# A scan and gated feed-forward kernel: w_down and one token slab loaded by GpSimd's queue instead of SyncE's

## The chip, the cores and the metric

The kernel runs on 1 core of one Trainium2 chip. A core has five engines with queues of their own: TensorE (PE, matmuls), VectorE (DVE), ScalarE (ACT), GpSimd (POOL) and SyncE (SP), and 16 DMA engines that move data between the chip's main memory and the on-chip buffer. The metric is the device time of one execution in microseconds (us). A profile shows one execution, with its times counted from the start of its span.

## The reference

For 2048 tokens x of 512 channels, in bf16:

```
xn = (x - mean) / sqrt(var + 1e-5)                       # over the 512 channels
h_t = Lam_bar * h_(t-1) + xn_t @ B_bar                   # complex, 512 states, t = 0..2047
s  = 2 * real(h @ C^T) + xn * Dskip
g  = silu((gelu(xn @ w_gate) * (xn @ w_up)) @ w_down)    # 512 -> 1376 -> 512
out = x + s * g
```

Lam_bar and B_bar come from Lambda, B and log_dt. The time loop is a recurrence over all tokens; the feed-forward part has no order among tokens.

## The kernel before, in words

The tokens are cut into 4 slabs (s = 0..3) of 512, each of 4 tiles (m = 0..3) of 128 tokens. For a slab:

- Tokens lie in x_tok. ScalarE normalizes them into xna (L749; for slab 0 VectorE does it at L356), with row scales rs made by GpSimd: L288 and L289 once for each tile of slab 0, L737 and L738 for slab 1, L761 for slabs 2 and 3. One DMA transpose (L360) turns xna into xnT.
- The scan half, `half(s, h)`: PE multiplies xnT by BT (L532, four matmuls for each of 8 groups), ScalarE copies each group out of its PSUM bank (L534, into U), VectorE rotates, scans (L563) and rotates back into hst. BT holds the transposed real and imaginary parts of B, loaded by two DMA transposes at L236. In the order of the program, slab 0's first three groups use the real part alone, and the fourth is the first to use the imaginary part.
- The feed-forward half: PE multiplies by w_up and w_gate (L402 and L383 in slab 0, L434 afterwards), ScalarE applies gelu, VectorE forms the product `at`, a DMA transpose (L450) puts it into atT, one for each tile, and PE multiplies atT by w_down, held in wd (L466, 11 matmuls a tile, `down_pair`). For slab 0 the tiles of atT are transposed, and used by PE, in the order 0, 2, 1, 3.
- `y_tile(s - 1, m)`: PE multiplies hst by the scaled C (L482); VectorE multiplies by g (L487), adds x (L493); SP stores the rows (L498).

PSUM has 6 ring banks shared by most products, and two banks for y_tile. A product waits until its bank's former contents were read.

Loads. All large DMAs go through SP's queue, in SP's order: first the tokens of slab 0 and the weights w_up and w_gate (L213 and L222), then the last rows of w_down (L669, 96 KB), slab 1's tokens (L217), Drow (L670), and the transposes of BT and of slab 0's xna. Behind slab 0's first atT come the other rows of w_down (L668, 1280 KB: 10 rows of 1 KB for each partition) and the tokens of slab 2 (L217, 512 KB), then the other transposes of atT. GpSimd issues no DMA; ScalarE issues three tiny ones at the start.

Order. Each operation is a step added by `pl.add`; `Plan.run` emits them in the order of the list `ORDER`, so that each engine's queue has its steps in that order. The arguments svc, dma, rank, lag and the costs are planning data and are not used when the kernel is built. An engine takes its own queue strictly in order, and a step that waits holds those behind it.

Of the kernel before, what the change touches and what calls it, by code (L numbers as in the profile page):

```python
# [17 lines left out]
PE, ACT, DVE, POOL, SP = "PE", "ACT", "DVE", "POOL", "SP"  # L18
# [2 lines left out]
ORDER = (  # L21
    20, 21, 22, 23, 24, 0, 26, 25, 19, 17, 18, 16, 1, 39, 14, 15, 12, 13, 2, 41, 3, 4, 5, 27, 28, 29, 30, 33, 60, 32, 46, 45, 40, 61, 34, 31, 63, 42,
    65, 62, 64, 69, 68, 66, 67, 70, 71, 72, 73, 35, 36, 37, 50, 51, 52, 54, 48, 53, 49, 57, 56, 58, 137, 38, 6, 43, 44, 147, 7, 79, 76, 82, 74, 80,
    77, 81, 78, 75, 8, 95, 91, 85, 97, 86, 93, 87, 88, 92, 55, 84, 47, 138, 94, 83, 96, 198, 149, 199, 151, 135, 59, 98, 136, 153, 9, 103, 107, 99,
    101, 109, 111, 104, 119, 100, 115, 102, 117, 108, 110, 125, 123, 133, 131, 216, 220, 139, 217, 140, 106, 120, 90, 112, 127, 214, 221, 105, 116,
    134, 154, 218, 150, 113, 126, 118, 124, 89, 215, 114, 128, 219, 122, 141, 148, 121, 143, 222, 223, 129, 130, 142, 152, 10, 155, 160, 164, 179,
    161, 165, 224, 229, 144, 11, 162, 166, 181, 183, 163, 185, 227, 167, 226, 225, 180, 168, 169, 170, 172, 171, 173, 174, 175, 176, 177, 178, 156,
    132, 233, 275, 283, 280, 279, 182, 358, 186, 184, 234, 187, 158, 237, 238, 276, 282, 157, 235, 228, 241, 243, 258, 244, 259, 236, 277, 278, 281,
    284, 285, 159, 239, 245, 296, 264, 247, 240, 246, 292, 260, 242, 200, 201, 202, 265, 302, 262, 297, 311, 293, 261, 298, 248, 303, 317, 307, 204,
    188, 203, 205, 263, 300, 294, 312, 308, 322, 299, 301, 315, 326, 313, 295, 309, 189, 191, 286, 190, 192, 230, 206, 207, 208, 318, 352, 316, 330,  # L30
    332, 232, 231, 305, 304, 327, 341, 209, 210, 211, 310, 324, 314, 328, 331, 323, 337, 290, 325, 339, 345, 287, 329, 288, 289, 333, 146, 320, 193,
# [5 lines left out]
    372, 486, 493, 501, 497, 474, 373, 484, 384, 385, 388, 386, 387, 467, 368, 434, 537, 477, 523, 494, 519, 478, 498, 487, 495, 524, 499, 525, 526,  # L37
    520, 507, 483, 389, 468, 390, 488, 374, 489, 504, 391, 505, 392, 401, 402, 403, 405, 406, 449, 551, 539, 521, 508, 552, 522, 513, 514, 535, 538,
    536, 515, 509, 404, 408, 407, 409, 527, 528, 531, 530, 518, 532, 469, 485, 464, 553, 490, 506, 557, 555, 541, 558, 569, 563, 556, 540, 559, 542,
    554, 565, 561, 567, 564, 578, 619, 562, 560, 574, 570, 624, 625, 576, 620, 584, 575, 568, 566, 580, 577, 591, 585, 599, 582, 589, 583, 597, 579,  # L40
    593, 581, 595, 572, 598, 600, 614, 510, 529, 516, 533, 571, 491, 587, 621, 629, 630, 612, 511, 622, 586, 626, 635, 615, 594, 596, 610, 608, 592,
    590, 604, 606, 636, 613, 607, 609, 605, 611, 534, 543, 544, 617, 601, 545, 573, 517, 627, 512, 602, 631, 470, 649, 616, 547, 548, 546, 549, 550,
    637, 623, 588, 643, 641, 644, 603, 645, 628, 638, 632, 618, 647, 650, 648, 655, 656, 642, 651, 661, 662, 646, 666, 667, 671, 672, 639, 640, 633,
    634, 652, 657, 658, 663, 664, 668, 669, 673, 674, 653, 654, 659, 660, 665, 670, 675,
)


# [33 lines left out]
def kernel(  # L81
# [17 lines left out]
    nc = tc.nc  # L99
# [9 lines left out]
    NS = S // TS  # L109
    M = TS // P  # L110
    NFT = (F + P - 1) // P
# [3 lines left out]
    HD = D // 2  # L115
# [12 lines left out]
    def sb(name, shape, dt=BF16):  # L128
        return consts.tile(shape, dt, name=name)

    x_tok = sb("x_tok", [P, NS * M, D])
# [3 lines left out]
    wd = sb("wd", [P, NFT, D])  # L135
# [43 lines left out]
    def dve(n, emit, reads=(), writes=(), rate=1.0, base=DV, **kw):  # L179
        return pl.add(DVE, base + n / 960.0 / rate, emit, reads, writes, lag=0.13, **kw)  # L180

    def acts(n, emit, reads=(), writes=(), ptr=0, **kw):
        return pl.add(ACT, AC + 0.12 * ptr + n / 1200.0, emit, reads, writes, lag=0.16, **kw)

    def pe(n, cols, emit, reads=(), writes=(), **kw):
        return pl.add(PE, n * (cols + 6) / 2400.0, emit, reads, writes, lag=0.22, **kw)
# [4 lines left out]
    def dma(eng, issue, land, emit, reads=(), writes=(), **kw):  # L191
        return pl.add(eng, issue, emit, reads, writes, lag=land, **kw)

    TURN, SLAB = (3, 2.28, 1.5), (2, 1.5, 1.0)
    x_r = A_x[0].rearrange("(m p) d -> p m d", p=P)
# [6 lines left out]
    sp_last, sp_at = [], [0.72]  # L202
# [11 lines left out]
               [(nm, k, c) for k in range(k0, k1) for c in range(3) if c0 <= CH[c][0] < c1])  # L214

    def load_slab(s, **kw):
        dma(SP, 0.8, 4.0, lambda: nc.sync.dma_start(out=x_tok[:, s * M : (s + 1) * M, :], in_=x_r[:, s * M : (s + 1) * M, :]),  # L217
            writes=[("x", s, m) for m in range(M)], svc=SLAB, **kw)


    def load_x(m, end, landed):
# [13 lines left out]
    for ri, src in enumerate((A_B_re, A_B_im)):  # L235
        dma(SP, 2.0, 3.0, lambda ri=ri, src=src: nc.sync.dma_start_transpose(out=BT[:, ri, :, :], in_=src), writes=[("BT", ri)],  # L236
            after=list(sp_last), svc=TURN)
# [16 lines left out]
    for i, (t, v) in enumerate(((pv0[0:4, :], A_log_dt), (pv1[0:4, :], A_Lambda_im), (pv1[4:8, :], A_Lambda_re))):  # L254
        first = [dma(ACT, 0.48, 1.7, lambda t=t, v=v: A.dma_start(out=t, in_=v.rearrange("(k p) -> k p", p=P)),
                     writes=[("pv", i)], rank=900.0, not_before=0.8, after=first)]
# [216 lines left out]
    def y_part(s, m, c0, c1, bank, key, seed, e):  # L473

        w = c1 - c0
        ps = bank[:, 0:w]
        if seed:
            acts(w, lambda: act(out=ps, in_=sk[s % 2][:, m, c0:c1], func=AF.Copy), [("sk", s % 2, m)], [key])  # L478

        def f():  # L480
            for j in range(2 * NPT):
                T.matmul(ps, lhsT=hst[s % 2][:, j // NPT, j % NPT, m * P : (m + 1) * P], rhs=C2[:, j // NPT, j % NPT, c0:c1],  # L482
                         start=(j == 0 and not seed), stop=(j == 2 * NPT - 1), skip_group_check=True)
        pe(2 * NPT, w, f, [("hst", s % 2, 0), ("hst", s % 2, 1)] + C2S + ([key] if seed else []), [key])
        gi, b = g2s[s, m]
        if seed:
            dve(w, lambda: V.tensor_tensor(out=yg[e][:, c0:c1], in0=ps, in1=g2[gi][:, b, c0:c1], op=ALU.mult), [key, ("g2", gi, b)], [("yg", e, c0)])  # L487
        else:
            ys = tF[:, 0, c0:c1]
            dve(w, lambda: V.tensor_tensor(out=ys, in0=ps, in1=sk[s % 2][:, m, c0:c1], op=ALU.add), [key, ("sk", s % 2, m)], [("tF",)])  # L490
            dve(w, lambda: V.tensor_tensor(out=yg[e][:, c0:c1], in0=ys, in1=g2[gi][:, b, c0:c1], op=ALU.mult), [("tF",), ("g2", gi, b)], [("yg", e, c0)])
        o = 2 + m % 2 if s == NS - 1 and m >= M - 2 else m % 2
        dve(w, lambda: V.tensor_tensor(out=ot[o][:, c0:c1], in0=yg[e][:, c0:c1], in1=x_tok[:, s * M + m, c0:c1], op=ALU.add),  # L493
            [("yg", e, c0), ("x", s, m)], [("ot", o, c0)], rate=2.0)
        mg = s * TS + m * P
        cuts = (0, HD) if (NS - 2, M - 2) <= (s, m) < (NS - 1, M - 2) else (c0,)
        for lo, hi in zip(cuts, (*cuts[1:], c1)):
            dma(SP, 0.35, 1.5, lambda lo=lo, hi=hi: nc.sync.dma_start(out=out_td[mg : mg + P, lo:hi], in_=ot[o][:, lo:hi]), [("ot", o, c0)], [("out", s, m, lo)], svc=(2, 0.4, 0.9))  # L498

    def y_tile(s, m):  # L500
        i = y_n[0] % 2
        seed = True
        y_n[0] += 1
        if (s, m) == (NS - 1, M - 1):
            for h in range(2):
                r, ps = bank()
                y_part(s, m, h * HD, (h + 1) * HD, ps, ("bank", r), True, m % 2)
        else:
            y_part(s, m, 0, D, ybank[i], ("y", i), seed, m % 2)
# [154 lines left out]
    for m in range(M):  # L664
        first_gates(m)
    load_slab(1, after=sp_last)
    wd_r = B_w_down[0 : (NFT - 1) * P, :].rearrange("(k p) d -> p k d", p=P)
    dma(SP, 0.6, 6.7, lambda: nc.sync.dma_start(out=wd[:, 0 : NFT - 1, :], in_=wd_r), writes=["wd0"], after=sp_last, svc=(2, 3.7, 1.0))  # L668
    dma(SP, 0.5, 4.0, lambda: nc.sync.dma_start(out=wd[:FL, NFT - 1, :], in_=B_w_down[(NFT - 1) * P : F, :]), writes=["wd"], after=sp_last, svc=(2, 0.3, 1.0))  # L669
    dma(SP, 0.7, 3.0, lambda: nc.sync.dma_start(out=Drow[:], in_=A_Dskip.partition_broadcast(P)), writes=["Drow"], after=sp_last, svc=(2, 0.5, 1.0))  # L670
    tables()
# [42 lines left out]
    for pt in range(NPT):  # L714
# [3 lines left out]
            out=C2[:, 0, pt, :], in0=CT[:, 0, pt, :], scalar=cre[:, pt : pt + 1], in1=tF[:, 1, :], op0=ALU.mult, op1=ALU.subtract),  # L718
            ["coef", ("CT", 0), ("tF",)], [("C2", 0, pt)], base=0.13)
        dve(512, lambda pt=pt: V.scalar_tensor_tensor(  # L720
            out=C2[:, 1, pt, :], in0=CT[:, 1, pt, :], scalar=ncre[:, pt : pt + 1], in1=tF[:, 0, :], op0=ALU.mult, op1=ALU.subtract),
# [104 lines left out]
```

## Time and profile before

| | us |
|---|---|
| median of 3 runs | 179.11 |
| lowest, highest | 178.77, 179.53 |
| the profiled execution, whole | 179.47 |
| its span | 177.7 |
| PE busy in the span | 172.0 |
| VectorE busy | 156.3 |
| ScalarE busy | 125.4 |
| GpSimd busy | 12.0 |

The profiled execution has 1.8 us outside its span. TensorE's granted clock was 1.00 all through. "Busy" of PE counts pipelined matmuls. In lines of the timeline the first column is the start, the second the duration of the group (for a DMA, of the issue on its queue, not of the transfer), then engine, line, operation, output and input; a bracket gives the idle time before the group and what ended it. "SPq" is SP's own instruction queue. A line of waits has the total, the number and the longest.

### The profile page before, as it was taken

How to read it: one execution, taken by the hardware profiler on the slowest of the kernel's cores; microseconds unless marked ns; L12 is line 12 of the kernel's file. 1: busy time of each engine (PE TensorE's matmuls, PEld its weight loads, DVE VectorE, ACT ScalarE, POOL GpSimd, SP SyncE). 2: the span in 40 equal slices, each digit the busy share in tenths (PEclk: the TensorE clock that was granted, in tenths of full speed). 3: DMA queues.
4: the chain of work that ended last, by engine and by line, in shares of the span. 5: the costliest groups of instructions: out<-in, count | busy, mean ns of one | idle time of the engine just before them, and what ended most of it. 6: DMA issues, size and time to landing. Idle time of an engine off the chain costs nothing.

```text
span 177.7 us, 2414 instructions
## 1 busy us (share of the span) xinstructions
PE 172.0 (97%) x834; PEld 82.4 (46%) x850; DVE 156.3 (88%) x252; ACT 125.4 (71%) x240; POOL 12.0 (7%) x25
## 2 busy tenths in 40 slices
PE   8999999899999999999999999999999999999992
PEld 2555544344455544444445454444444455444451
DVE  3729999999598994999979999899999999999754
ACT  6789999797998999899578855373148618572240
POOL 2471040000200000000040000000000000000000
PEclk9999999999999999999999999999999999999999
DMA  5999999999000709414000075094000006527022
GB/s 149 351 374 201 167 247 308 172 203 207 0 0 0 190 10 181 103 59 81 0 0 6 18 112 129 29 193 85 0 0 0 0 30 151 75 50 143 21 78 78
DMA packets 48083, 18.66 MB, mean 105 GB/s; under 512 B 40296, under 2 KB 47048, under 8 KB 48072
## 3 DMA queue, kind: packets, MB, share of 16 engines
q1 hardware_dynamic: 48048, 18.52, 49.0%
q8 instruction: 6, 0.10, 0.3%
q14 instruction: 5, 0.04, 0.1%
q10 hardware_dynamic: 24, 0.00, 0.0%
HBM read 6.46 MB, written 2.10 MB: 48 GB/s over the span
## 4 chain that ended last, share of the span: by engine, by line
PE 81%; DVE 8%; DMA 6%; ACT 2%; issue 1%; POOL 0%; DVEq 0%
PE ring L434 31%; PE ring L466 20%; PE ybank L482 14%; PE ring L532 12%; DMA atT<-at 5%; PE ring L383 3%; ACT at L392 2%; DVE st L279 1%; DVE Q L624 1%; DMA x_tok<-in_A_x_dram 1%; DVE at L416 1%; DVE yg L487 1%; DVE tab L624 1%; DVE junk L493 1%; DVE sk L365 1%
## 5 line engine op out<-in xcount | busy, mean ns | idle before, releaser
L434 PEld LDWEIGHTS <-xnT 128*128 128x128 bf16 x288 | 28.2, 98 | 28.4
L466 PE MATMUL ring<-wd,atT 128*128 128x512 bf16 (+1 forms) x170 | 39.0, 379 | 1.1 <-DMA atT<-at 0.7
L434 PE MATMUL ring<-wg,xnT 128*128 128x512 bf16 (+1 forms) x143 | 31.4, 357 | 0.1
L434 PE MATMUL ring<-wu,xnT 128*128 128x512 bf16 (+1 forms) x141 | 31.2, 356 | 0.2
L532 PE MATMUL ring<-xnT,BT 128*128 128x512 bf16 x128 | 30.1, 379 | 0.0
L563 DVE TENSOR_TENSOR_SCAN Fs<-rho,ini,W 128x512 bf16<-128x512 f32 x24 | 29.7, 1270 | 0.1
L437 ACT ACTIVATE ub<-ring 128x512 bf16<-128x512 f32 (+1 forms) x36 | 19.2, 555 | 14.1 <-PE ring L434 14.0
L482 PE MATMUL ybank<-C,hst 128*128 128x512 bf16 x116 | 27.3, 379 | 0.2
L466 PEld LDWEIGHTS <-atT 128*128 128x128 bf16 (+1 forms) x176 | 17.1, 98 | 22.0 <-DMA atT<-at 1.2
L534 ACT ACTIVATE U<-ring 128x512 bf16<-128x512 f32 x32 | 18.3, 601 | 8.1 <-PE ring L532 8.1
L437 ACT ACTIVATE gt<-ring 128x512 bf16<-128x512 f32 (+1 forms) x36 | 19.5, 556 | 3.7 <-PE ring L434 3.5
L482 PEld LDWEIGHTS <-hst 128*128 128x128 bf16 x136 | 13.3, 98 | 14.0
L532 PEld LDWEIGHTS <-BT 128*128 128x128 bf16 x128 | 12.5, 98 | 14.7
L544 DVE TENSOR_TENSOR Q<-U,tab 128x4096 bf16<-128x4096 bf16 x8 | 18.3, 2290 | 1.0 <-ACT tab L631 0.7
L469 ACT ACTIVATE g<-ring 128x512 f32<-128x512 f32 x16 | 9.3, 594 | 13.6 <-PE ring L466 13.5
L544 DVE TENSOR_TENSOR Q<-Fs,tab 128x4096 bf16<-128x4096 bf16 x8 | 18.3, 2287 | 0.1
L487 DVE TENSOR_TENSOR yg<-ybank,g 128x512 bf16<-128x512 f32 x15 | 10.2, 685 | 5.4 <-PE ybank L482 5.3
L744 ACT ACTIVATE junk<-x_tok 128x512 bf16<-128x512 bf16 x16 | 10.0, 635 | 1.1 <-DMA x_tok<-in_A_x_dram 1.1
L478 ACT ACTIVATE ybank<-sk 128x512 f32<-128x512 bf16 x15 | 9.0, 602 | 1.7 <-DVE yg L487 1.6
L749 ACT ACTIVATE xna<-x_tok,nb,rs 128x512 bf16<-128x512 bf16 x12 | 9.6, 817 | 0.0
L402 PE MATMUL ring<-wg,W 128*128 128x512 bf16 (+1 forms) x47 | 9.4, 356 | 0.1
L563 DVE TENSOR_TENSOR_SCAN Fs<-rho,W 128x512 bf16<-128x512 f32 x8 | 9.3, 1210 | 0.1
(127 smaller groups left out, 170.5 us busy)
## 6 DMA issues: line engine op xcount, KB each, us to landing
x_tok<-in_A_x_dram SPq DMA_DIRECT2D x3, 512.0 KB, 9.0
wg<-in_B_w_gate_dram SPq DMA_DIRECT2D x1, 1376.0 KB, 8.5
wd<-in_B_w_down_dram SPq DMA_DIRECT2D x1, 1280.0 KB, 8.2
out_dram<-ot SPq DMA_DIRECT2D x10, 128.0 KB, 1.7
wu<-in_B_w_up_dram SPq DMA_DIRECT2D x4, 256.0 KB, 4.0
x_tok<-in_A_x_dram SPq DMA_DIRECT2D x4, 128.0 KB, 2.3
out_dram<-ot SPq DMA_DIRECT2D x8, 64.0 KB, 1.6
wu<-in_B_w_up_dram SPq DMA_DIRECT2D x1, 352.0 KB
```

What stands on the lines that cost most here:

```text
L402: T.matmul(ps[:, 0 : b - a], lhsT=xcT[:, k, m * P : (m + 1) * P], rhs=wt[:, k, a:b], start=(k == 0), stop=(k == KT - 1))
L434: T.matmul(ps[:, 0 : b - a], lhsT=xnT[:, s % 2, m, k, :], rhs=wt[:, k, a:b], start=(k == 0), stop=(k == KT - 1))
L437: acts(b - a, lambda: act(out=dst[:, a:b], in_=ps[:, 0 : b - a], func=AF.Copy if up else AF.Gelu_apprx_tanh), [("bank", r)], [key], table= ...
L466: T.matmul(ps[:], lhsT=atT[:fs, k, m * P : (m + 1) * P], rhs=wd[:fs, k, :], start=(k == 0), stop=(k == NFT - 1))
L482: T.matmul(ps, lhsT=hst[s % 2][:, j // NPT, j % NPT, m * P : (m + 1) * P], rhs=C2[:, j // NPT, j % NPT, c0:c1], start=(j == 0 and not seed ...
L487: dve(w, lambda: V.tensor_tensor(out=yg[e][:, c0:c1], in0=ps, in1=g2[gi][:, b, c0:c1], op=ALU.mult), [key, ("g2", gi, b)], [("yg", e, c0)])
L532: T.matmul(ps[:], lhsT=BT[:, ri, k, pt * P : (pt + 1) * P], rhs=xnT[:, s % 2, :, k, :], start=(k == 0), stop=(k == KT - 1))
L534: acts(512, lambda q=q, ri=ri, ps=ps: act(out=U[ui][:, ri, q, :], in_=ps[:], func=AF.Copy), [("bank", r)], [("U", ui, q, ri)])
L544: dve(4096, lambda: V.tensor_tensor(out=Qf, in0=src.unsqueeze(1).to_broadcast(WQ), in1=table, op=ALU.mult), reads, ["Q"], rate=2.0)
L563: pl.add(DVE, 1.12 if s == 0 else 1.185, lambda ri=ri, q=q, pt=pt, first=first: V.tensor_tensor_scan(out=Fs[:, ri, q, :], data0=rho[:, pt ...
L744: acts(512, lambda i=i, fn=fn, sc=sc, m=m: act(out=junk()[:], in_=x_tok[:, s * M + m, :], func=fn, scale=sc, accum_out=sx[:, s, i, m : m + ...
L749: acts(512, lambda m=m: act(out=xn[m], in_=x_tok[:, s * M + m, :], func=AF.Identity, scale=rs[:, s, m : m + 1], bias=nb[:, s, m : m + 1]), ...
```

## The change

- The load of w_down's first 1280 rows (`wd`, before at L668) and the load of slab 2's tokens are issued by GpSimd instead of SP. In `ORDER` their steps (132 and 275) stand directly behind step 153, slab 0's last row scale, and so in GpSimd's queue between the L289 of tile 3 and the L737 and L738 of slab 1. In SP's queue they are gone from between the first and the second atT of slab 0.
- The stores of tiles 0 and 1 of slab 2 are issued in two halves of 256 columns each, as those of the four tiles after them already were. SP's queue has two stores more for it.
- No other instruction changes its place on its engine, nor do the waits other than by the new number of the semaphores. One added line shifts the line numbers by one. Slabs 1 and 3 stay on SP.

```diff
 ORDER = (
...
-  ... 59, 98, 136, 153, 9, 103, 107, ...
+  ... 59, 98, 136, 153, 132, 275, 9, 103, 107, ...
...
     def load_slab(s, **kw):
-        dma(SP, 0.8, 4.0, lambda: nc.sync.dma_start(out=x_tok[:, s * M : (s + 1) * M, :], in_=x_r[:, s * M : (s + 1) * M, :]),
-            writes=[("x", s, m) for m in range(M)], svc=SLAB, **kw)
+        eng, nq = (POOL, nc.gpsimd) if s == 2 else (SP, nc.sync)
+        dma(eng, 0.8, 4.0, lambda: nq.dma_start(out=x_tok[:, s * M : (s + 1) * M, :], in_=x_r[:, s * M : (s + 1) * M, :]),
+            writes=[("x", s, m) for m in range(M)], dma=(2, 0.8, 1.5), **kw)
...
-        cuts = (0, HD) if (NS - 2, M - 2) <= (s, m) < (NS - 1, M - 2) else (c0,)
+        cuts = (0, HD) if NS * M - 8 <= s * M + m < NS * M - 2 else (c0,)
...
-    dma(SP, 0.6, 6.7, lambda: nc.sync.dma_start(out=wd[:, 0 : NFT - 1, :], in_=wd_r), writes=["wd0"], after=sp_last, svc=(2, 3.7, 1.0))
+    dma(POOL, 0.6, 6.7, lambda: nc.gpsimd.dma_start(out=wd[:, 0 : NFT - 1, :], in_=wd_r), writes=["wd0"], after=sp_last, dma=(2, 0.8, 3.7))
```

## The prediction

> **What bounds the kernel now.** I read the page first: busy time by engine, and the DMA line of the 40 slices.
>
> ```profile
> PE 172.0 (97%) x834; PEld 82.4 (46%) x850; DVE 156.3 (88%) x252; ACT 125.4 (71%) x240; POOL 12.0 (7%) x25
> ...
> DMA  5999999999000709414000075094000006527022
> ```
>
> TensorE (PE) is busy in 172.0 of 177.7 us, and the DMA engines are full from 4.4 to 44 us (nine slices of 4.44 us), which is where the change works. Next I asked who waited on PE; the whole answer is two lines.
>
> ```profile
> PE ybank L296 <- PEq L810: 0.8, 1, 0.8
> PE ring L466 <- DMA atT<-at: 0.7, 1, 0.7
> ```
>
> The first is the start. The second is the only stall after it. PE's timeline from 17 us shows where:
>
> ```profile
> 24.11 7.07 PE L532 MATMUL ring<-xnT,BT 128*128 128x512 bf16 x32
> 31.22 2.54 PE L466 MATMUL ring<-wd,atT 128*128 128x512 bf16 x10
> 34.46 4.93 PE L466 MATMUL ring<-wd,atT 128*128 128x512 bf16 x22 [0.71 <-DMA atT<-at]
> ```
>
> From 34.46 PE runs without a gap to 172.7 us; the last stores end the span at 177.7. So a stall put in before 34 us is paid in full at the end, and the most that loads can give back is 0.71 us. What feeds this stretch is SP's queue and, in the changed kernel, POOL's. SP's timeline (start, duration of the issue):
>
> ```profile
> 15.61 3.08 SPq L360 DMA_TRANSPOSE xnT<-xna  x1
> 18.74 2.20 SPq L236 DMA_TRANSPOSE BT<-in_A_B_im_dram  x1
> 21.04 1.92 SPq L450 DMA_TRANSPOSE atT<-at  x1
> 23.01 0.58 SPq L668 DMA_DIRECT2D wd<-in_B_w_down_dram  x1
> 23.63 0.70 SPq L217 DMA_DIRECT2D x_tok<-in_A_x_dram  x1
> 25.21 8.34 SPq L450 DMA_TRANSPOSE atT<-at  x2
> 33.65 2.17 SPq L360 DMA_TRANSPOSE xnT<-xna  x1
> ```
>
> POOL's, around the new place of the two loads, which is behind the L289 of 14.64:
>
> ```profile
> 14.64 0.55 POOL L289 TENSOR_TENSOR rs<-ve,mhalf 128x1 f32<-128x1 f32 x1
> 22.98 0.24 POOL L737 TENSOR_SCALAR mq<-mv 128x4 f32<-128x4 f32 x1 [7.78 <-DVE mv L280]
> 23.30 1.84 POOL L738 TENSOR_TENSOR rs<-mq,mhalf 128x4 f32<-128x4 f32 x1
> ```
>
> And the windows of one us (last columns: DMA share, GB/s):
>
> ```profile
> 18.00:19.00 1.00, 1.00 (x6) 1.00 0.15 24
> 19.00:20.00 1.00, 1.00 (x9) 1.00 1.27 290
> 20.00:21.00 1.00, 1.00 (x7) 1.00 1.10 202
> ...
> 24.00:25.00 1.00, 1.00 (x7) 1.00 0.64 130
> ...
> 27.00:28.00 1.00, 1.00 (x7) 1.00 0.99 338
> ```
>
> Transposes move 240 GB/s (mean of the five windows from 19 to 24), plain loads 334 (mean of 26 to 30), and the engines are nearly empty from 18 to 19. From the issues and their times to landing: xnT of slab 0 lands at 15.61 + 6.1 = 21.7, BT's second half (BT_im) at 18.74 + 4.9 = 23.6, wd at 23.01 + 8.2 = 31.2, atT of token tile 2 at 25.21 + 9.2 = 34.4, slab 2 at about 32.5 (ScalarE's L744 waits 1.14 us and starts at 32.58).
>
> **Part 1: the stall that goes.** atT of tile 2 was queued at 25.21 behind wd and slab 2, 1.8 MB. Its issue stays at 25.21: SP waited there for VectorE's product, which ends at 25.19, so the 0.58 and 0.70 us of SP time saved bring nothing. Without that queue it lands in 3.5 to 4.1 us (the other atT rows), at about 29.3, before PE asks at 33.75. Gain: 0.71 us. Next late would be tile 1's atT, due at 33.76 + 2.54 = 36.3; it was in time even behind the queue. ScalarE's 1.14 us wait for slab 2 goes too, worth 0, since PE never waits for ScalarE in this trace. wd itself was due at 31.22 and landed at 31.2; moved up it has room.
>
> **Part 2: the stall that may come.** POOL reaches the loads at 15.19 (end of L289; neither waits for anything). Their bytes flow from about 16.2 (estimate: half of the 2.13 us from the first load's issue at 0.72 to its landing at 2.85). From then on they share the 16 DMA engines with the rest of BT_re, with xnT and with BT_im, which before had them alone. Who waits: the first matmul of L532 needs xnT at 24.11, slack 24.11 - 21.7 = 2.4. In program order three groups of four L532 matmuls use only BT_re, the fourth is the first with BT_im: at 24.11 + 3 x 0.864 = 26.70, slack 3.1.
>
> The work: BT_re has about 0.28 MB left at 16.2 (the 229 and 100 GB/s windows of 16 to 18), 1.2 us at 240 GB/s. xnT and BT_im are 0.524 MB each, 2.2 us each. Check on before: xnT's issue ends at 18.69; 18.69 + 2.2 + 2.2 + 0.55 to land = 23.64, as seen. The plain 1.83 MB need 5.5 us at 334 GB/s. No row of before has two queues with heavy traffic, so I bound it by how the engines might be shared:
> - No slowing, transposes leave gaps enough: stall 0.
> - Equal bytes: each side gets 1/(1/240 + 1/334) = 140 GB/s, a transpose takes 3.75 us. From 18.69, xnT lands at 23.0 (in time), BT_im at 18.69 + 7.5 + 0.55 = 26.75: stall 0.05.
> - Equal time: a transpose takes 4.4 us. xnT lands at 23.65 (in time), BT_im at 28.0: stall 1.3.
> - Plain loads first: 16.2 + 5.5 + 1.2 + 2.2 + 0.55 = 25.65 for xnT: stall 1.5; BT_im at 27.85 is then in time (due 28.24).
> - Plain first at the price they had in SP's queue, 7.3 us (atT of tile 0 landed about 25.2, slab 2 at 32.5): xnT at 27.45, stall 3.3.
>
> I take 1.0, between equal bytes and equal time but nearer the latter: the one issue made under plain traffic, the first of the two atT at 25.21, took 2.62 us where the same issue alone takes 1.40, so slowing by about two is what a row shows. Range of this term 0 to 3.3.
>
> The Trainium skill, "DMA: Bandwidth & Descriptors", section "Issuing engines are not separate DMA queues", says that transfers started by different engines run on the same 16 DMA engines and interleave, and that a second issuing engine saves only issue time. By that rule the no-slowing end falls away and the sum lies at the equal-bytes row or above.
>
> **Part 3: POOL's time.** Issuing on POOL is not in the trace. Low bound: SP's own issues of these two, 0.58 + 0.70 = 1.28 us; high bound: the longest issue in the trace twice, BT_re's 7.54 us, 15.1. Behind the loads on POOL stand L737 and L738, slab 1's row scales; ScalarE's L749 waits for those, and behind it in ScalarE's order the L534 copies that free PE's banks. Cover: POOL sat idle 7.8 us from 15.19 to 22.98. Then the third L534 ends at 28.37, and PE wants its bank for the eighth L532 group at 24.11 + 7 x 0.864 = 30.16: another 1.8. Up to 9.6 us for both issues cost nothing; I take the low end (same loads, nearest row), so 0.
>
> **Part 4: stores in halves.** Tiles 8 and 9 (slab 2) get one more SP issue each, 0.33 to 0.78 us (store rows after 140 us), ahead of slab 3's atT of tiles 1 and 3. The later of these is issued at 160.37 and lands 3.5 us on, at 163.9; PE wants it as its fourth down tile at 158.0 + 3 x 2.38 = 165.1. Slack 1.2 against at most 0.78: cost 0. Without that cover it would cost up to 0.78.
>
> **Sum.** The profiled execution took 179.47 us, 177.7 of span and 1.8 around it; that is 0.36 above the median of 179.11, so I apply differences to the median. -0.71 + 1.0 + 0 + 0 = +0.3: 179.4 us, a span near 178.0.
>
> **The rivals.**
> A, the loads slip in unseen. For it: the empty windows at 18 and 24. Against: everything else from 15 to 25 shows a DMA share at or above 1. Stall 0 to 0.4, time 178.4 to 178.8. More than 0.71 it cannot give, as PE has no other gap.
> B, transposes suffer more than by two. For it: BT_re's issue took 7.54 us while wg, slab 1 and others drained ahead of it; that queueing could return across queues. Against: its own queue was the full one there. Stall 1.6 to 3.3: 180.0 to 181.7.
> C, slower by POOL: writing requests for 1280 + 512 rows holds POOL past 24.8 us. It decides from 9.6 us for both issues. At 15.1, POOL gets to L737 at 30.3, the scales are ready at 32.5, L749 and the third L534 end at 34.2: PE's eighth group waits 4.0 and the second down tile 0.3 more for the fifth L534. -0.71 + 4.3 = +3.6: 182.7. Against it: SP's issue of these very loads took 1.28.
> D, VectorE keeps POOL from writing the requests while it works. VectorE runs from 15.23 to 30.2 almost without a gap; loads that start at 30.2 put wd at 30.2 + 8.2 = 38.4 where PE wants it at 31.22: +7.2 - 0.71, or 185.6. Against it: L738 ran wholly beside VectorE's work and was stretched to 1.84 us, from the 1.01 that L761's same operation took; it was not held to the end of that work. The Trainium skill warns of such a hold in "SBUF — State Buffer", section "SBUF: two separate sides": a 2-port VectorE operation locks GpSimd out while it writes descriptors. [...]
>
> **How the numbers follow.** A measurement of this kernel can tell about 0.5%, 0.9 us: 178.2 to 180.0 is no change. Forecast, stall 0.4 to 1.6, 178.8 to 180.0: 0.37, all within. A 0.25, of which 0.06 is measured more than 0.9 faster (the three runs of before scatter by 0.76) and 0.19 within. B 0.21, C 0.13 and D 0.04, all slower. Faster 0.06, same 0.56, slower 0.38. The range goes from A's end less scatter, 178.3, to B's end, 181.8; outside lie the low part of A, most of C and D, together under 0.2.
>
> **What would show it.** Right: wd and slab 2 land before 29 us; no PE wait at L466; one PE wait of about 1 us at L532, for xnT or BT_im; L737 still near 23.0. No wait at L532 is A; one above 1.6 is B; a late L737 with ScalarE waiting at L749 is C; wd landing after 31 is D. Wrong altogether: a new gap on PE after 40 us, or a tail that moves by more than 0.3 us.

## The result, and the profile after

| | before | after |
|---|---|---|
| median, us | 179.0 (6 runs, 178.77 to 179.53) | 185.37 (6 runs, 183.7 to 187.94) |
| profiled execution, us | 179.47 | 185.53 |
| its span, us | 177.7 | 183.7 |

The ratio is 1.031, with a 95% interval of 1.026 to 1.036: slower by 5.5 us, where the prediction said 179.4 and at most 181.8. Ratios leave out executions more than 1.5% above the fastest of their kernel (here 187.22 and 187.94), medians do not: by the medians it is 6.4 us.

The page of the changed kernel: the engines (busy, share, instructions), TensorE's granted clock in 40 slices of 4.59 us, the two DMA queues (packets, MB, share of 16 engines), and the two moved loads with the time from issue to landing.

```profile
PE 175.1 (95%) x850; PEld 83.3 (45%) x850; DVE 156.3 (85%) x252; ACT 125.3 (68%) x240; POOL 13.9 (8%) x27
...
PEclk9999997899999999999999999999999999999999
...
q1 hardware_dynamic: 46512, 16.68, 43.6%
q0 software_dynamic: 480, 1.84, 3.6%
...
wd<-in_B_w_down_dram POOLq DMA_DIRECT2D x1, 1280.0 KB, 11.1
...
x_tok<-in_A_x_dram POOLq DMA_DIRECT2D x1, 512.0 KB, 11.5
```

PE is busy for longer, 175.1 instead of 172.0 us. A part of this is the clock, which is low in the seventh and eighth slices, 27.6 to 36.7 us; another part may be missing records, since the profile before has 834 of the 850 matmuls. GpSimd's queue is a queue of its own, q0, and the profile calls it a software queue; SP's transposes and stores are q1.

PE's waits after (total, number, longest; the line numbers are higher by one than before):

```profile
PE ring L533 <- DMA xnT<-xna: 4.6, 1, 4.6
PE ybank L297 <- PEq L811: 0.8, 1, 0.8
```

The stall at w_down (0.7 us before) is gone; in its place stands one for xnT of slab 0, of 4.6 us. PE's timeline after:

```profile
29.49 8.75 PE L533 MATMUL ring<-xnT,BT 128*128 128x512 bf16 x32 [4.58 <-DMA xnT<-xna]
38.08 7.30 PE L467 MATMUL ring<-wd,atT 128*128 128x512 bf16 x33
45.22 2.75 PE L533 MATMUL ring<-xnT,BT 128*128 128x512 bf16 x12
```

Two things to see: the 32 matmuls begin at 29.49 instead of 24.11, and they take 8.75 us instead of 7.07. From 38 us PE runs without a gap. SP's queue and GpSimd's after (start, duration of the issue):

```profile
16.24 6.31 SPq L361 DMA_TRANSPOSE xnT<-xna  x1
22.60 6.36 SPq L237 DMA_TRANSPOSE BT<-in_A_B_im_dram  x1
29.06 4.93 SPq L451 DMA_TRANSPOSE atT<-at  x3
```
```profile
15.78 1.18 POOL L669 DMA_DIRECT2D wd<-in_B_w_down_dram  x1
16.96 0.78 POOL L218 DMA_DIRECT2D x_tok<-in_A_x_dram  x1
23.61 0.24 POOL L738 TENSOR_SCALAR mq<-mv 128x4 f32<-128x4 f32 x1 [5.88 <-DVE mv L281]
```

xnT's issue takes 6.31 us (3.08 before) and xnT lands 13.1 us after its start, at 29.4 (6.1 and 21.7 before). wd lands at 15.78 + 11.1 = 26.9, slab 2 at 16.96 + 11.5 = 28.5. The windows of one us of the changed kernel (length, PE busy and its matmuls, granted clock, DMA share, GB/s):

```profile
17.00:18.00 1.00, 1.00 (x7) 1.00 0.36 63
18.00:19.00 1.00, 1.00 (x6) 1.00 1.74 115
19.00:20.00 1.00, 1.00 (x8) 1.00 0.90 121
20.00:21.00 1.00, 1.00 (x8) 1.00 0.59 196
21.00:22.00 1.00, 1.00 (x7) 1.00 1.00 337
...
26.00:27.00 1.00, 0.00 (x0) 1.00 1.47 111
27.00:28.00 1.00, 0.00 (x0) 1.00 1.26 44
...
31.00:32.00 1.00, 1.00 (x4) 0.50 1.10 200
32.00:33.00 1.00, 1.00 (x4) 0.50 1.06 205
33.00:34.00 1.00, 1.00 (x6) 0.85 1.16 207
```

PE is idle from 26 to 28 (0.00, no matmul). The DMA engines move little at both ends of the loads, 63 to 196 GB/s from 17 to 21 us and 111 and 44 from 26 to 28, and PE's clock is at half from 30 to 33.

**Where the 6.0 us of span went.** 0.64 is in the head: the same L384 group starts at 6.37 instead of 5.73, before any changed instruction has run, so it is scatter. The first scan matmul comes at 29.49, 4.74 later than 24.11 + 0.64. From it to the next slab's first L533 (45.22) it is 15.73 us, 15.12 before: 0.61 more. The scan group takes 1.48 more to the first L467 (8.59 for 7.11), the slow clock; from there on it is 0.87 less, the 0.71 stall and some small gaps. The sum is 5.99; PE's last group starts at 178.53 instead of 172.54, which is 5.99 too.

### The profile page after: what moved, and what is told of

The parts are those of the page before. It is cut to its first block, busy times and chain, and to the rows that moved or that the text cites. A ratio compares the mean times of both kernels' runs of the same rounds, so it can differ in the third digit from the quotient of the medians.

```text
span 183.7 us, 2435 instructions
## 1 busy us (share of the span) xinstructions
PE 175.1 (95%) x850; PEld 83.3 (45%) x850; DVE 156.3 (85%) x252; ACT 125.3 (68%) x240; POOL 13.9 (8%) x27
## 3 DMA queue, kind: packets, MB, share of 16 engines
q0 software_dynamic: 480, 1.84, 3.6%
## 4 chain that ended last, share of the span: by engine, by line
PE 87%; DMA 7%; ACT 2%; DVE 2%; POOL 0%; issue 0%; DVEq 0%
PE ring L435 30%; PE ring L467 21%; PE ring L533 16%; PE ybank L483 14%; DMA xnT<-xna 7%; PE ring L384 3%; ACT at L393 2%; PE ring L297 1%; DVE yg L488 1%; PE ybank L297 1%; DVE junk L494 1%; ACT junk L353 0%; PE ybank L329 0%; PE ring L314 0%; POOL rs L290 0%
## 5 line engine op out<-in xcount | busy, mean ns | idle before, releaser
L467 PE MATMUL ring<-wd,atT 128*128 128x512 bf16 (+1 forms) x176 | 39.3, 379 | 0.0
L533 PE MATMUL ring<-xnT,BT 128*128 128x512 bf16 x128 | 31.8, 395 | 4.6 <-DMA xnT<-xna 4.6
L564 DVE TENSOR_TENSOR_SCAN Fs<-rho,ini,W 128x512 bf16<-128x512 f32 x24 | 29.7, 1270 | 0.1
L438 ACT ACTIVATE ub<-ring 128x512 bf16<-128x512 f32 (+1 forms) x36 | 19.2, 555 | 14.1 <-PE ring L435 14.0
L467 PEld LDWEIGHTS <-atT 128*128 128x128 bf16 (+1 forms) x176 | 17.2, 98 | 20.8
L533 PEld LDWEIGHTS <-BT 128*128 128x128 bf16 x128 | 12.9, 101 | 20.8 <-issue 7.3
L366 DVE TENSOR_TENSOR sk<-xna,Drow 128x512 bf16<-128x512 bf16 x16 | 6.5, 412 | 4.7 <-ACT xna L750 4.7
## 6 DMA issues: line engine op xcount, KB each, us to landing
wd<-in_B_w_down_dram POOLq DMA_DIRECT2D x1, 1280.0 KB, 11.1
x_tok<-in_A_x_dram POOLq DMA_DIRECT2D x1, 512.0 KB, 11.5
```

Of the source, the lines that this page charges most:

```text
L438: acts(b - a, lambda: act(out=dst[:, a:b], in_=ps[:, 0 : b - a], func=AF.Copy if up else AF.Gelu_apprx_tanh), [("bank", r)], [key], table= ...
L467: T.matmul(ps[:], lhsT=atT[:fs, k, m * P : (m + 1) * P], rhs=wd[:fs, k, :], start=(k == 0), stop=(k == NFT - 1))
L533: T.matmul(ps[:], lhsT=BT[:, ri, k, pt * P : (pt + 1) * P], rhs=xnT[:, s % 2, :, k, :], start=(k == 0), stop=(k == KT - 1))
L564: pl.add(DVE, 1.12 if s == 0 else 1.185, lambda ri=ri, q=q, pt=pt, first=first: V.tensor_tensor_scan(out=Fs[:, ri, q, :], data0=rho[:, pt ...
```

## Experiments

The first theory was the prediction's own, that transposes and loads share the 16 engines; its rivals were the stores in halves, GpSimd's issue time, the kind of queue, and the clock. Times are medians, ratios are to the kernel before on the same chip with their 95% intervals. An edit is shown against the kernel before, but that of `e4_act_queue`, `e6_pool_late`, `e7_after_fill`, `e9_slab3_pool` and `e13_after_fill26` against the changed kernel, that of `e8_act_big` against `e4_act_queue`, and that of `e11_wd_first` against `e10_slab_behind`. The change's stores in halves are in `e1_halves`, `e7_after_fill`, `e12_after_again` and `e13_after_fill26` alone.

### The parts by themselves

**Stores in halves alone** (`e1_halves`): the changed kernel with both loads back in their places on SP. Against the kernel before:

```diff
-        cuts = (0, HD) if (NS - 2, M - 2) <= (s, m) < (NS - 1, M - 2) else (c0,)
+        cuts = (0, HD) if NS * M - 8 <= s * M + m < NS * M - 2 else (c0,)
```

> Kernel before with the two more stores in halves only; both loads stay on SP. Theory 1 (the loads on GpSimd's queue get ahead of xnT's transpose on the shared DMA engines; the stores do nothing): 179.0 us within 0.5, PE's waits as before (0.7 at L466). Theory 2 (GpSimd's software queue itself, whatever its load, is what costs): the same, 179.0. A part of the 5 us from the stores would show here as a new wait or a longer tail after 140 us.

Measured: 179.25 us, ratio 1.0017 [0.9997, 1.0037]. The stores cost nothing that can be told.

**wd alone on GpSimd's queue** (`e2_wd_pool`): step 132 behind 153, slab 2 stays on SP.

```diff
-    dma(SP, ... nc.sync.dma_start(out=wd[:, 0 : NFT - 1, :], ...
+    dma(POOL, ... nc.gpsimd.dma_start(out=wd[:, 0 : NFT - 1, :], ...
```

> Kernel before with only wd's load (1.31 of the 1.83 MB) moved to GpSimd behind slab 0's row scales. Theory 1: xnT's landing moves by the bytes ahead of it, 7.0 x 1.31/1.83 = 5.0 us against 2.4 us of slack: PE waits about 2.6 us at L532, total 181 to 182 us. Theory 2: a cost that belongs to the queue and not to the bytes, so the same 4.6 us wait and 184 us as with both loads.

Measured: 183.55 us, ratio 1.0226 [1.0162, 1.029]. PE's waits in its profile (of an execution of 184.88 us, longer than the median):

```profile
PE ring L532 <- DMA xnT<-xna: 4.0, 1, 4.0
```

wd by itself makes most of the wait, in this execution more than the 2.6 us that its share of the bytes would give.

**Slab 2 alone on GpSimd's queue** (`e3_slab_pool`): step 275 behind 153, wd stays on SP.

```diff
-        dma(SP, ... nc.sync.dma_start(out=x_tok[...
+        eng, nq = (POOL, nc.gpsimd) if s == 2 else (SP, nc.sync)
+        dma(eng, ... nq.dma_start(out=x_tok[...
```

> Kernel before with only slab 2's load (0.52 of the 1.83 MB) moved to GpSimd. Theory 1: xnT moves by 7.0 x 0.52/1.83 = 2.0 us, inside its 2.4 us of slack: no wait at L532, and the 0.7 us wait at L466 shrinks, since tile 2's atT stands behind wd alone: 178.2 to 179.0 us. Theory 2: the same wait at L532 as with both loads, above 182 us.

Measured: 180.36 us, ratio 1.0075 [1.0046, 1.0103]. PE's waits, and the packets by queue between 20 and 22 us:

```profile
PE ring L467 <- DMA wd<-in_B_w_down_dram: 2.3, 1, 2.3
```
```profile
q1 hardware_dynamic: 48, 0.01, 47.4%
q0 software_dynamic: 9, 0.03, 6.0%
```

xnT is in time (15.98 + 8.4 = 24.4), but its issue still holds SP for 6.23 us. So SP issues wd at 26.09 instead of 23.01, it lands at 33.9, and PE waits for that. For two us in which xnT is under way only 48 of its packets end, while nine stragglers of the software queue finish.

### The same bytes in other queues

**Both loads on ScalarE's queue**, issued at 15.7 and 16.1 us (`e4_act_queue`):

```diff
-        eng, nq = (POOL, nc.gpsimd) if s == 2 else (SP, nc.sync)
+        eng, nq = (ACT, nc.scalar) if s == 2 else (SP, nc.sync)
...
-    dma(POOL, ... nc.gpsimd.dma_start(out=wd[:, 0 : NFT - 1, :], ...
+    dma(ACT, ... nc.scalar.dma_start(out=wd[:, 0 : NFT - 1, :], ...
```

> Kernel before with both loads issued at nearly the same time (about 16.5 us) by ScalarE's hardware queue instead of GpSimd's software queue. Theory 1 in its plain form (all packets take turns, 1 KB rows against transposes of under 512 B): xnT lands late here too, PE waits 1 to 5 us at L532, 180 to 184 us; if the size of a packet decides (480 packets for 1.84 MB on the software queue are 3.8 KB each), the wait is shorter than the 4.6 us on GpSimd. Theory 2: no wait at L532, 178.4 us.

Measured: 180.84 us, ratio 1.0101 [1.0071, 1.013]. Its waits and PE's timeline:

```profile
PE ring L533 <- DMA xnT<-xna: 1.9, 1, 1.9
```
```profile
26.68 7.07 PE L533 MATMUL ring<-xnT,BT 128*128 128x512 bf16 x32 [1.93 <-DMA xnT<-xna]
```

The same bytes at the same time cost 1.9 us of waiting instead of 4.6, and the clock stays at 1.00 (32 matmuls in 7.07 us). This is near "plain loads first" (1.5) of the prediction's list, not equal bytes.

**Both loads on SP's queue, between BT_re and xnT** (`e5_sp_early`), so with no second queue. Against the kernel before:

```diff
-  ... 152, 10, 155, ...    156, 132, 233, 275, 283, ...
+  ... 152, 10, 132, 275, 155, ...    156, 233, 283, ...
```

> Kernel before with both loads still on SP, but between BT_re and xnT of slab 0, so that they go ahead of xnT in one queue, with no second queue at all. Bytes ahead are the whole cost (theory 1 as first stated): the loads take 5.5 to 7.3 us, xnT lands near 28 to 29 as in the changed kernel, PE waits 3.5 to 4.6 us at L532, 182.5 to 184 us. If instead two queues at once cost more than their bytes (xnT's issue took 6.2 us in every run with a second queue, and the windows from 17 to 20 us moved 63 to 196 GB/s), this kernel is quicker than the changed one: xnT lands near 16.2 + 5.5 + 2.2 + 1 = 25 to 26, PE waits 1 to 2 us, about 180 to 181 us.

Measured: 182.03 us, ratio 1.0174 [1.0117, 1.0231]; the profiled execution took 181.35. Its waits:

```profile
PE ring L532 <- DMA xnT<-xna: 1.9, 1, 1.9
```

Loads that stand outright in front of xnT, in its own queue, make PE wait as long as ScalarE's queue does, and less than half as long as GpSimd's in the changed kernel. The profiled execution is the shortest of four; what makes the others 0.6 to 2.1 us longer is not shown.

**ScalarE's queue with large packets** (`e8_act_big`): each partition reads one run of 10 KB (wd) or, by the same edit, of 4 KB (slab 2). The tiles then hold other rows than the reference asks for, so that only the times of this run are of use.

```diff
-    wd_r = B_w_down[0 : (NFT - 1) * P, :].rearrange("(k p) d -> p k d", p=P)
+    wd_r = B_w_down[0 : (NFT - 1) * P, :].rearrange("(p k) d -> p k d", p=P)
```

> As the kernel with both loads on ScalarE's hardware queue, but each partition reads one contiguous run from memory (10 KB of w_down, 4 KB of the slab), which puts other rows of w_down and of the tokens into the tiles than the reference has; the bytes and the tiles' shapes are the same. If the size of the packets decides how far xnT falls behind: with large packets on the hardware queue PE waits at L532 as on GpSimd, 3.5 us or more, 182 to 184 us. If it is the software queue as such: as with 1 KB rows on ScalarE's queue, a wait near 1.9 us, 180.8 us.

Measured: 180.72 us, ratio 1.0094 [1.0063, 1.0124], a wait of 1.8 us: as `e4_act_queue`. The size of the packets is not what sets the software queue apart.

Those three runs and the changed kernel, asked for the packets of each queue, show how the engines are shared (packets that ended, MB, share of 16 engines, which passes 100% where packets overlap). The changed kernel, 17 to 21 us, then 22 to 24, then 26 to 28:

```profile
q0 software_dynamic: 84, 0.34, 61.3%
q1 hardware_dynamic: 527, 0.13, 26.1%
...
q0 software_dynamic: 172, 0.67, 95.4%
q1 hardware_dynamic: 170, 0.04, 10.8%
...
q1 hardware_dynamic: 364, 0.09, 128.2%
q0 software_dynamic: 22, 0.06, 8.3%
```

ScalarE's queue (q10), `e4_act_queue`, 17 to 21 us, then 22 to 24:

```profile
q10 hardware_dynamic: 975, 1.00, 94.9%
q1 hardware_dynamic: 458, 0.11, 15.8%
...
q10 hardware_dynamic: 555, 0.55, 79.2%
q1 hardware_dynamic: 551, 0.14, 31.6%
```

And `e8_act_big`, 21 to 23 us:

```profile
q10 hardware_dynamic: 109, 0.42, 88.4%
q1 hardware_dynamic: 106, 0.03, 14.9%
```

The kernel before, 22 to 23 us, with transposes alone:

```profile
q1 hardware_dynamic: 1145, 0.29, 127.5%
```

Where both queues have work the packets go one for one: 172 to 170, 555 to 551, 109 to 106. A transpose's packet holds 256 bytes (0.04 MB in 170), a load's 1 KB to 4 KB. So the transposes get 6% of the bytes in the changed kernel and 20% in `e4_act_queue`: the loads go first in all but name. The Trainium skill, "DMA: Bandwidth & Descriptors", section "SWDGE vs HWDGE vs iDMA", says that software and hardware queues feed different queues inside a DMA engine, which takes turns between them; the equal counts agree, and show that the turn is a packet.

The software queue's further 2.7 us lies before and behind that stretch. It moved 0.34 MB from 17 to 21, ScalarE's 1.00. And its end is slow: from 26 to 28 some 22 stragglers are left, the transposes do 364 packets in two us where they do 1145 in one when alone (before, 22 to 23), and as the last straggler ends (28 us) the rate is back at 890. In `e4_act_queue` xnT lands 2.8 us earlier (26.6 against 29.4). These 2.7 us are one execution's: from its issue to its landing xnT took 13.1 us there, and 11.5 to 14.1 in three other profiles with both loads in this place (`e12_after_again`, `e13_after_fill26`, `e7_after_fill`).

**Slab 3's load on GpSimd's queue** at 47.44 us, when the engines have nothing else (`e9_slab3_pool`), wd and slab 2 on SP as before:

```diff
-        eng, nq = (POOL, nc.gpsimd) if s == 2 else (SP, nc.sync)
+        eng, nq = (POOL, nc.gpsimd) if s == 3 else (SP, nc.sync)
```

> Kernel before with only slab 3's load (0.52 MB) moved from SP to GpSimd, behind slab 2's row scales, so issued near 47 us, when nothing else is moved. It measures the software queue alone. If the software queue is slow by itself: 0.52 MB take clearly more than the roughly 2 us of bytes that an SP load of the same size shows when alone (windows of 60 to 63 us in the kernel before: 306 GB/s at best), and land 5 us or more after the issue. If it is slow only while transposes are moving: about 2 us of bytes near 300 GB/s, landing about 4 us after the issue. Total 179 us in both cases, since the slab is used far later.

Measured: 179.2 us in one execution. Its windows:

```profile
49.00:50.00 1.00, 1.00 (x7) 1.00 0.52 168
50.00:51.00 1.00, 1.00 (x7) 1.00 0.89 356
```

No byte moves before 49.25 us, 1.8 after the issue; then it is soon 356 GB/s, and the load lands 4.1 us after its issue, though VectorE is busy for 0.89 to 1.00 of each us from 47 to 51. The software queue alone is not slow in moving bytes: it is slow beside transposes.

### Another place on GpSimd's queue

**Both loads on GpSimd behind L738 and L739** (`e6_pool_late`):

```diff
-  ... 136, 153, 132, 275, 9, ...    143, 222, 223, ...
+  ... 136, 153, 9, ...    143, 222, 132, 275, 223, ...
```

> Kernel before with both loads on GpSimd, but behind slab 1's row scales (L738), so issued near 25 us, after xnT and BT_im have landed. If the place in time is the cause: no wait at L532 on xnT; wd lands near 25 + 8 to 10 = 33 to 35, so PE waits 2 to 4 us at the first L466 instead, 180 to 182 us. If GpSimd's software queue costs something of its own apart from xnT: above 183 us, or a wait elsewhere.

Measured: 183.33 us, ratio 1.02 [1.0151, 1.025]. Its GpSimd timeline and PE's waits (of an execution of 186.85 us, longer than the median, so read for the order of events):

```profile
23.49 3.44 POOL L738 TENSOR_SCALAR mq<-mv 128x4 f32<-128x4 f32 x1 [7.78 <-DVE mv L281]
...
28.01 1.18 POOL L669 DMA_DIRECT2D wd<-in_B_w_down_dram  x1
```
```profile
PE ring L467 <- DMA wd<-in_B_w_down_dram: 5.5, 1, 5.5
```

xnT is in time here, and wd is late instead: issued at 28.01, landed 9.1 us on, at 37.1. GpSimd's 0.24 us operation took 3.44 in this execution, which made the loads later still. Of the two places tried on this queue one is too early for xnT, the other too late for wd.

### The clock

**20 filler matmuls ahead of the first scan matmul** (`e7_after_fill`), else the changed kernel:

```diff
+                    for _ in range(20 if s == 0 and pt == 0 and ri == 0 else 0):
+                        T.matmul(ps[:], lhsT=warm[:, 0:P], rhs=warm, start=True, stop=True)
```

> The changed kernel with 20 extra matmuls on a constant (20 x 0.216 = 4.3 us) ahead of the first L532 group, in the bank which that group then overwrites, so that PE works while xnT is late. If the halved clock from 30 to 33 us in the changed kernel comes from PE's idle 4.6 us: the clock stays at 1.00, the 32 matmuls of L532 take 6.9 us instead of 8.75, and the total falls by about 1.8 us, to 182 to 183.5. If the clock falls for another reason: no change from the changed kernel, or slower.

Measured: 184.3 us, ratio 1.0305 [1.0254, 1.0356]. The clock stays at 1.00 and the 32 matmuls take 7.07 us, but the changed kernel was not run on this chip, so its price could not be told. Hence the pair, on one chip: **the changed kernel again** (`e12_after_again`, no edit) and **26 fillers** (`e13_after_fill26`, `range(26 ...` in the line above).

> The changed kernel again, unaltered, as the partner of the next run on the same chip. Expected 183.7 to 185.5 us, a wait of 4 to 5 us at L533 for xnT, the clock near 0.5 for about 3.4 us behind it.

> The changed kernel with 26 filler matmuls (5.6 us) ahead of the first L533 group, which covers the whole wait. If idling lowers the clock and the lowered clock costs about 1.8 us: 1.0 to 1.8 us less than the changed kernel on this chip (less, where xnT lands before the fillers end), the clock 1.00 throughout, L533's 32 matmuls in 7.1 us. If the lowered clock costs nothing that matters: equal or up to 1 us slower than the changed kernel, by the fillers that run too long.

Measured: 185.72 us (185.1 to 186.66) and 184.68 (184.03 to 184.98), ratios 1.036 [1.0304, 1.0415] and 1.0293 [1.0255, 1.0331]. PE's timelines, the first without fillers, the second with:

```profile
29.82 8.75 PE L533 MATMUL ring<-xnT,BT 128*128 128x512 bf16 x32 [2.96 <-DMA xnT<-xna]
```
```profile
24.97 5.85 PE L533 MATMUL ring<-const-bfloat16-1.0 128*128 128x512 bf16 x26
30.66 7.07 PE L535 MATMUL ring<-xnT,BT 128*128 128x512 bf16 x32
```

Useless work makes the kernel 1.0 us faster, though the fillers end some 0.4 after xnT's landing (16.47 + 13.8 = 30.3). In these two traces the scan group takes 1.7 us less up to the first L467 (8.59 and 6.91). So of the 6 us some 1 to 1.7 is the clock, and most of the rest the late xnT. The wait in `e12_after_again` is 2.96 and not the 4 to 5 expected: there the products ahead of it end 1.95 us later than in the changed kernel's first profile (26.87 against 24.92), while xnT lands at 18.19 + 11.5 = 29.7, much as before (29.4).

### Without a second queue

**Slab 2 on SP behind the atT of tile 2** (`e10_slab_behind`), whose step is 158. Against the kernel before:

```diff
-  ... 132, 233, 275, 283, ...    187, 158, 237, ...
+  ... 132, 233, 158, 275, 283, ...    187, 237, ...
```

> Kernel before with slab 2's load still on SP, but behind the atT transpose of tile 2 instead of ahead of it. By the account of the stall in the kernel before (atT of tile 2 queued behind 1.8 MB): it lands 1.5 us sooner, the 0.7 us wait at L466 goes, slab 2 lands about 2 us later, which delays only ScalarE: 178.2 to 178.7 us, ratio 0.995 to 0.998. If slab 2's lateness reaches PE through ScalarE's order (L744 ahead of the sixth L534 copy): 179 to 180 us.

Measured: 178.72 us, ratio 0.9993 [0.9968, 1.0019]. PE's timeline has the 33 down matmuls in one piece:

```profile
31.36 7.30 PE L466 MATMUL ring<-wd,atT 128*128 128x512 bf16 x33
```

The 0.71 stall is gone from this profile (span 176.9), but the time does not show it. Nor is slab 2's place shown as its cause: with slab 2 in the old place the stall is 0.2 us in `e1_halves`, and `e9_slab3_pool` has none:

```profile
31.74 7.30 PE L467 MATMUL ring<-wd,atT 128*128 128x512 bf16 x33
```

The atT of tile 2 lands 9.2 us after its issue in the kernel before, 8.8 and 7.5 in those two: the stall varies with the execution.

**wd ahead of tile 0's atT too** (`e11_wd_first`); 156 is that atT:

```diff
-  ... 178, 156, 132, 233, 158, 275, ...
+  ... 178, 132, 156, 233, 158, 275, ...
```

> As the last kernel, and wd's load moved ahead of atT of tile 0 in SP's queue, behind BT_im. wd lands about 2 us sooner than 31.2, atT of tile 0 behind it, near 30.5, where PE asks for both at 31.2; the remaining small gaps ahead of 39 us (about 0.5 us in all beside the 0.7) may close: 178.0 to 178.7 us. If atT of tile 0 lands later than 31.2: a new wait of up to 1 us at the first L466 and 179 to 179.7 us.

Measured: 179.64 us, ratio 1.0029 [1.0004, 1.0054], with a new wait for atT at L466 of 0.8 us in the profiled execution, the longest of twelve. No version ran measurably faster than the kernel before.

## Why the prediction was wrong

**The step that failed is the size of Part 2's term.** Its mechanism was the right one: the loads delay xnT at the first L532. It took 1.0 us, between equal bytes (0.05) and equal time (1.3), and its upper bound was 3.3. The wait measured 4.6. The row that set the 1.0 was misread (in 1), and three things were missed.

1. *The rule of sharing.* The engines share by packets, one for one, which none of the bounds was. With 256 bytes against 1 KB or more that is close to "plain loads first", 1.5 in the list; where nothing else was different (`e4_act_queue`, `e5_sp_early`, `e8_act_big`) the wait was 1.8 to 1.9. The 1.0 was chosen by a row that was misread: of the two atT issues at 25.21 (8.34 us in one merged row) the first, made under plain traffic, took 5.72 us and not 2.62, which is the second. SP's timeline of the kernel before, from 24 to 27 us, has it by itself:

```profile
25.21 5.72 SPq L450 DMA_TRANSPOSE atT<-at  x1
```

So the row showed slowing by four, against 1.40 alone, and not by two. Used as the prediction used two, four gives an estimate of 18.69 + 4 x 2.2 + 0.55 = 28.0 for xnT, a wait of 3.9. That would be near by luck: it is the time of an issue and not a share of bytes, and twice too much for the same loads on ScalarE's queue (1.9). The rule from the Trainium skill that the prediction weighed, interleaving on the same engines, held; by itself it prices no delay.
2. *The kind of queue.* Work was taken as conserved: so many bytes at 334 or 240 GB/s, from 16.2 us on. In the software queue the first packets of the loads ended after 18 us, and slow stretches beside the transposes, ahead and behind, took another 2.7 us of waiting in the profiled execution. No row of before has a software queue that could have priced that. `e9_slab3_pool` excludes the queue alone, `e8_act_big` the packet size. What makes the transposes crawl while its last packets finish is open; a shorter crawl (77 GB/s at 26 to 27 us) also appears in `e5_sp_early`, where no such packets are.
3. *The clock.* The sum had no term for it. After 4.6 us of idle PE the granted clock is at half for some 3.4 us (three whole windows, 0.3 of the one behind, 0.1 of the one ahead), and that costs 1.0 or more (`e12_after_again` against `e13_after_fill26`). An idle of 1.9 us (`e4_act_queue`, `e5_sp_early`) leaves it at 1.00, one of 2.96 (`e12_after_again`) does not. The Trainium skill, "TensorE: Matmul & The Clock Gate", section "Part 1: The HAM clock gate (the "warmup" mystery)", gives half clock after an idle window of about 3.4 us, and full clock after a busy one as long. The length at half agrees; the idle that brings it on was shorter here, and the measurement decides.

**Point by point.**
- Part 1 came out in the changed kernel's profile, which has no wait for atT at w_down's matmuls. But the 0.71 us were one execution's, and `e10_slab_behind` gains nothing that can be told.
- Part 2's second check point, the fourth group's need of BT_im, did not matter: xnT alone was late enough. BT_im landed at 22.60 + 8.5 = 31.1, and the matmuls that need it did not wait.
- Part 3 was right: the two issues took 1.18 + 0.78 = 1.96 us against a cover of 9.6, and L738 at 23.61 waits for VectorE, not for the loads. Rival C is false.
- Part 4 was right (`e1_halves`).
- Of the signs, wd and slab 2 did land before 29, and L466 has no wait; the wait at the first scan group was not "about 1" but above 1.6, which the text had named as rival B. B ended at 181.7 because its dearest bound kept SP's price for the loads and a full clock (181.8 in the range is the same sum, a tenth off).
- Rival D is false as put: wd landed at 26.9, beside VectorE's work and not after it.
- What no part had: loads ahead of it double the time for which xnT's issue holds SP, 3.1 to 6.3 us here, much as the issue of 5.72 us above. It cost nothing in the changed kernel, where PE was late already, but 2.3 us in `e3_slab_pool`.

## What to carry to other kernels

Before a load is moved to another queue, look up which DMA transposes will be under way, and what slack PE has for them: packets are taken in turns, so a transpose in 256-byte packets got 6% of the bytes beside packets of 3.9 KB and 20% beside those of 1 KB. Price a software queue beside transposes at more than its bytes, or keep it for stretches where the engines are empty. Where a sum gives a wait of PE of 3 us or more, add the half clock that follows. And where a row of a timeline merges two issues, ask for each by itself before a price is taken from it.

## What the hardware showed that was not expected

- Two queues with work share the DMA engines by equal counts of packets: 172 to 170, 555 to 551 and 109 to 106, with load packets of 1 KB as of 3.9 KB.
- The software queue moved nothing for some 2 us after the start of its issue, then 356 GB/s when alone (`e9_slab3_pool`); it joined rows of 1 KB into packets of 3.8 KB (480 for 1.84 MB).
- xnT's issue on SP went from 3.1 to between 5.3 (`e7_after_fill`) and 7.3 us (`e8_act_big`) in the runs with loads in a second queue ahead of it, and to 7.4 with the loads ahead in its own (`e5_sp_early`).
- A GpSimd operation of 0.24 us took 3.44 in two executions (`e6_pool_late`, `e13_after_fill26`). In both VectorE's row was full meanwhile, and it ended 0.1 us after VectorE's last operation there; that VectorE held it is not shown.
